# An adaLN block with linear attention and a gated feed-forward: a hand-interleaved kernel rewritten as a task graph ordered by a list scheduler

## Chip, cores and metric

One core of a Trainium2 chip. The metric is device time in microseconds (us) of one execution. Ratios in this text are the mean time of one kernel's fast runs over that of the other's of the same rounds, so not quite the ratio of the medians that are quoted. In the profile PE is TensorE, PEld its weight loads, DVE VectorE, ACT ScalarE, POOL GpSimd, SP SyncE.

## The reference, cut to what matters

```python
# x: (1, 2048, 512) bf16, 32 heads of 16, feed-forward width 1376
mod = silu(c) @ w_mod                                   # 6 vectors of 512: sa, ca, ga, sb, cb, gb
h   = layernorm(x) * (1 + ca) + sa
q, k, v = split(h @ wqkv)
pq, pk  = q @ w_phi, k @ w_phi                          # per head, 16x16
phi_q   = concat(softmax(pq), softmax(-pq))             # 32 features per head
phi_k   = concat(softmax(pk), softmax(-pk))
kv, z   = phi_k.T @ v, sum(phi_k)                       # over all 2048 positions
o   = (phi_q @ kv) / (phi_q @ z + 1e-6)
x   = x + ga * (o @ wo)
h   = layernorm(x) * (1 + cb) + sb
x   = x + gb * ((sigmoid(h @ w_gate) * (h @ w_up)) @ w_down)
```

kv needs every position, so no output tile can start before all 16 tiles (128 rows each) have been through K, V and phi. That cuts the kernel into stages: A, loads and preparation; B, the key/value pass over 16 tiles; C, the way from kv to the first gate matmul; D, the feed-forward part, during which the later tiles still pass through attention.

Names in the profiles: xn is a normalised tile, h1T and h2T its transposes with scale and shift; kvbd is kv laid out for the matmuls; sm, m, den and cc are the steps from phi_q @ z to the factor that divides, num is phi_q @ kv, u the divided num; a_ps is the product with `wo`, tg the tanh of gate, hm its product with up, y the product with `w_down`. To evict is to copy a result out of PSUM, TensorE's output memory of eight banks.

## The kernel before

`w_phi` is folded into the weights of q and k at the start; `ga` is multiplied into `wo`, and `gb` into `w_down`, on the chip. Everything is emitted in an order fixed by hand. Stage B is a loop over tiles with the preparation of the next group of four tiles woven in:

```python
    for i in range(NT):
        g, j = i // 4 + 1, i % 4
        k_v(i)                                   # V matmuls of tile i
        k_vaug(i)                                # ACT: evict V
        if j == 0 and g < 4:
            for t in range(4 * g, 4 * g + 4):
                ln1_xn(t)                        # DVE: normalise the next group
        k_k(i)                                   # K matmuls of tile i
        if g < 4:
            ln1_quarter(g, j, 7, on_dve=False)   # 4 TensorE transposes, ACT eviction
        # ... (cut)
        k_exp(i)                                 # ACT: exp(k), exp(-k)
        if i >= 3:
            k_kv(i - 3, kvacc, vaug[(i - 3) % VS])
        if i >= 1 and g < 3:
            ln_stats(x_sb[:, 4 * g + 4 + j, :], st1, mv1, 4 * g + 4 + j)
            if j == 3:
                ln_rstd(slice(4 * g + 4, 4 * g + 8), mv1, ve1, rs1)   # POOL
        # ... (cut)
        k_norm(i)                                # DVE: sum, reciprocal; POOL: phi
```

In stage D, chunks of 2, 2, 4, 4 and 4 tiles go through gate and up. Gate has PSUM bank 0 and up bank 1 (two of each in the first chunk), y banks 2 and 3, attention 4 to 7. After each slice of 128 features, a fixed number of y matmuls of the chunk before is issued, then those attention steps whose hand-set time has come:

```python
        for k, ct in enumerate(CHUNKS):
            # ... (cut)
            for ft in range(FT):
                gb_, ub_ = ((0, 1) if ft % 2 == 0 else (2, 3)) if k == 0 else (0, 1)     # (shortened)
                # gate matmuls -> ACT tanh -> up matmuls -> DVE hm
                if k == 0 and first:
                    wd_scale(ft)                 # POOL: gb into w_down
                # ... y matmuls of the chunk before: `per` of them
                run_events()                     # attention steps that are due
```

## Time and profile before

| | before |
|---|---|
| median of 4 runs beside the changed kernel | 281.55 us (281.06 to 281.93) |
| profiled span | 279.7 us |
| stage B ends (last kvacc matmul) | 85.1 us |
| first gate matmul | 110.8 us |
| last y done (last output addition starts) | 274.2 us |

How to read the page: the first part gives each engine's busy time in the span; the second cuts the span into 40 slices (7 us each here) and gives the busy share of each in tenths. PEclk is the clock granted to TensorE in tenths. These are lines of both parts for the kernel before:

```profile
span 279.7 us, 3972 instructions
PE 223.1 (80%) x1494; PEld 122.1 (44%) x1494; DVE 171.2 (61%) x330; ACT 104.9 (38%) x197; POOL 77.0 (28%) x85
...
PE   0959679399786757768777958999769899999992
...
DVE  2576876747358494869677866476957445942420
...
POOL 3432725727570040645722040103120100000000
PEclk9986959779999997979999999999999999999998
```

Where stage B ends is read from the timeline (start, length, then engine, line, operation, tiles, count); these are the eight kvacc matmuls of the sixteenth tile:

```profile
84.48 0.64 PE L245 MATMUL kvacc<-vaug,phi 128*128 128x136 bf16 x8
```

TensorE's row has 6s and 7s up to three quarters of the span, and its clock falls to 5 to 7 in several slices. The windows, the chain and the waits of this kernel are in the prediction.

### The profile page before, as it was taken

To read this page: it belongs to the slowest core of one execution; us is meant where nothing else is said; L and a number is where in the kernel's file an instruction comes from. 1 tells how busy PE (TensorE), PEld (TensorE's weight loads), DVE (VectorE), ACT (ScalarE), POOL (GpSimd) and SP (SyncE) were. 2 spreads that over 40 slices of the span, in tenths; PEclk is the share of its full clock that TensorE was granted. 3 is DMA by queue.
4 is the path that set the end of the run, shared out by engine and by line. 5 is a ranking of instruction groups with operands and counts; after the bars stand their busy time and mean duration, and the time that the engine had idled before them with its cause. 6 is when DMAs were issued, how large, how long until landed. Compare 5 with 4: busy or idle time off the path is not lost.

```text
span 279.7 us, 3972 instructions
## 1 busy us (share of the span) xinstructions
PE 223.1 (80%) x1494; PEld 122.1 (44%) x1494; DVE 171.2 (61%) x330; ACT 104.9 (38%) x197; POOL 77.0 (28%) x85
## 2 busy tenths in 40 slices
PE   0959679399786757768777958999769899999992
PEld 0814336155443434645455643445424344444440
DVE  2576876747358494869677866476957445942420
ACT  2637538168674534334443122431131322122100
POOL 3432725727570040645722040103120100000000
PEclk9986959779999997979999999999999999999998
DMA  7999900000000000001111203021022100000011
GB/s 201 397 290 406 363 6 1 0 0 2 0 1 2 0 0 2 0 5 35 39 38 23 73 2 95 0 56 41 0 55 57 40 20 19 19 21 19 20 57 45
DMA packets 23178, 17.14 MB, mean 61 GB/s; under 512 B 15617, under 2 KB 20594, under 8 KB 23154
## 3 DMA queue, kind: packets, MB, share of 16 engines
q1 hardware_dynamic: 23120, 16.82, 19.2%
q8 instruction: 13, 0.21, 0.3%
q14 instruction: 11, 0.09, 0.1%
q0 software_dynamic: 32, 0.02, 0.1%
q10 hardware_dynamic: 2, 0.00, 0.0%
HBM read 11.06 MB, written 2.10 MB: 47 GB/s over the span
## 4 chain that ended last, share of the span: by engine, by line
PE 54%; DVE 18%; issue 7%; POOL 6%; ACT 6%; DMA 5%; SPq 2%; POOLq 0%; DVEq 0%; ACTq 0%
PE y_ps L570 10%; PE g_ps L597 9%; PE u_ps L602 9%; PE v_ps L218 5%; PE k_ps L223 4%; PE a_ps L428 4%; PE q_ps L253 4%; PE kvacc L245 3%; DVE st L130 3%; DMA wp_sb<-in_A_w_phi_dram 2%; PE tp_h L147 2%; POOL phi L239 2%; DVE u L402 2%; POOL rs L135 2%; DVE xn L141 2%
## 5 line engine op out<-in xcount | busy, mean ns | idle before, releaser
L603 DVE SCALAR_TENSOR_TENSOR hm<-tg,u_ps 128x512 bf16<-128x512 bf16 (+3 forms) x55 | 31.7, 577 | 46.2 <-PE u_ps L602 33.2
L599 ACT ACTIVATE tg<-g_ps 128x512 bf16<-128x512 f32 (+3 forms) x55 | 28.0, 509 | 70.7 <-PE g_ps L597 68.3
L597 PE MATMUL g_ps<-h2T,wg_sb 128*128 128x512 bf16 (+3 forms) x220 | 47.5, 339 | 5.0 <-ACT tg L599 4.9
L602 PE MATMUL u_ps<-h2T,wu_sb 128*128 128x512 bf16 (+3 forms) x220 | 47.1, 337 | 4.3 <-DVE hm L603 4.1
L570 PE MATMUL y_ps<-wd_sb,hm 128*128 128x512 bf16 (+1 forms) x176 | 45.3, 379 | 0.0
L239 POOL TENSOR_TENSOR phi<-e,kr 128x1024 bf16<-128x1024 bf16 x16 | 30.8, 1927 | 29.9 <-DVE kr L237 21.8
L597 PEld LDWEIGHTS <-wg_sb 128*128 128x128 bf16 (+1 forms) x220 | 21.5, 101 | 24.0 <-issue 7.4
L602 PEld LDWEIGHTS <-wu_sb 128*128 128x128 bf16 (+1 forms) x220 | 21.9, 100 | 21.5 <-issue 5.3
L235 DVE TENSOR_REDUCE ksum<-e 128x64 f32<-128x1024 bf16 x16 | 19.3, 1208 | 18.0 <-ACT e L231 18.0
L409 POOL TENSOR_TENSOR o<-u,u 128x512 bf16<-128x512 f32 x12 | 15.2, 1266 | 44.4 <-DVE u L402 42.4
L570 PEld LDWEIGHTS <-hm 128*128 128x128 bf16 (+1 forms) x176 | 17.2, 98 | 18.4
L256 ACT ACTIVATE eT<-q_ps 128x512 bf16<-128x512 f32 x32 | 17.4, 595 | 16.9 <-PE q_ps L253 16.9
L428 PE MATMUL a_ps<-wo_sb,oT 128*128 128x512 bf16 x64 | 17.3, 394 | 7.5 <-ACT eT L256 2.6
L402 DVE TENSOR_TENSOR u<-num,cc 128x512 f32<-128x512 f32 (+1 forms) x32 | 20.4, 681 | 0.8 <-PE num L400 0.6
L218 PE MATMUL v_ps<-wv_sb,h1T 128*128 128x512 bf16 x64 | 20.1, 445 | 0.0
L134 POOL TENSOR_SCALAR ve<-mv 128x2 f32<-128x2 f32 (+1 forms) x12 | 2.7, 224 | 59.8 <-DVE mv L131 59.8
L152 ACT ACTIVATE h1T<-tp_h,modc 128x512 bf16<-128x512 bf16 x14 | 10.9, 779 | 21.8 <-PE tp_h L147 21.7
L223 PE MATMUL k_ps<-wqk_f,h1T 128*128 128x512 bf16 x64 | 19.0, 426 | 0.0
L147 PE MATMUL tp_h<-ident,xn 128*128 128x128 bf16 x64 | 9.6, 266 | 11.6 <-DVE xn L141 11.1
L253 PE MATMUL q_ps<-h1T,wqk_f 128*128 128x512 bf16 x64 | 18.2, 410 | 0.0
L231 ACT ACTIVATE e<-k_ps 128x512 bf16<-128x512 f32 x32 | 17.2, 595 | 0.2 <-PE k_ps L223 0.2
L447 ACT ACTIVATE xn<-x,nmr,rs 128x512 bf16<-128x512 f32 x12 | 9.4, 807 | 19.3 <-DVE nmr L440 19.3
(94 smaller groups left out, 269.0 us busy)
## 6 DMA issues: line engine op xcount, KB each, us to landing
x_sb<-in_A_x_dram SPq DMA_DIRECT2D x4, 512.0 KB, 9.8
wmod_sb<-in_w_mod_dram SPq DMA_DIRECT2D x1, 2048.0 KB, 8.7
out_dram<-ot SPq DMA_DIRECT2D x16, 128.0 KB, 1.7
wg_sb<-in_B_w_gate_dram SPq DMA_DIRECT2D x1, 1376.0 KB, 12.5
wu_sb<-in_B_w_up_dram SPq DMA_DIRECT2D x1, 1376.0 KB, 15.4
wd_sb<-in_B_w_down_dram SPq DMA_DIRECT2D x1, 1280.0 KB, 15.5
wmod_sb<-in_w_mod_dram SPq DMA_DIRECT2D x1, 1024.0 KB, 8.0
wk_sb<-in_A_wqkv_dram SPq DMA_DIRECT2D x1, 512.0 KB, 5.7
```

Of the source, the lines that this page charges most:

```text
L218: pe.matmul(v_ps[t][:], lhsT=h1T[:, j, t * P:(t + 1) * P], rhs=wv_sb[:, j, :], start=(j == 0), stop=(j == KT - 1))
L223: pe.matmul(k_ps[t][:], lhsT=h1T[:, j, t * P:(t + 1) * P], rhs=wqk_f[:, j, D:2 * D], start=(j == 0), stop=(j == KT - 1))
L235: dve.tensor_reduce(sm[:], e_t[t][:], axis=AX.X, op=ALU.add)
L239: pool.tensor_tensor(phi_t[t][:], e_t[t][:], r[:].unsqueeze(3).to_broadcast([P, 2, H, DH]), op=ALU.mult)
L253: pe.matmul(ps[:], lhsT=wqk_f[:, j, blk * P:(blk + 1) * P], rhs=h1T[:, j, cq * 512:(cq + 1) * 512], start=(j == 0), stop=(j == KT - 1))
L402: dve.tensor_tensor(u[:], ps[:].rearrange("p (h d) -> p h d", d=DH), c_t[p][:, q, s, :].unsqueeze(2).to_broadcast([P, H, DH]), op=ALU.mult)
L428: pe.matmul(ps[:], lhsT=o[:, j, :], rhs=wo_sb[:, j, :], start=(j == 0), stop=(j == KT - 1))
L570: yield lambda y=y, ft=ft, fsz=fsz, tl=tl: pe.matmul(y[:], lhsT=hm[k][:fsz, ft, tl * P:(tl + 1) * P], rhs=wd_sb[:fsz, ft, :], start=(ft == ...
L597: pe.matmul(g_ps[:fsz, 0:n], lhsT=wg_sb[:, j, ft * P:ft * P + fsz], rhs=h2T[k][:, j, 0:n], start=(j == 0), stop=(j == KT - 1))
L599: act.activation(tg[:fsz, 0:n], g_ps[:fsz, 0:n], ACT.Tanh, scale=0.5)
L602: pe.matmul(u_ps[:fsz, 0:n], lhsT=wu_sb[:, j, ft * P:ft * P + fsz], rhs=h2T[k][:, j, 0:n], start=(j == 0), stop=(j == KT - 1))
L603: dve.scalar_tensor_tensor(hm[k][:fsz, ft, 0:n], tg[:fsz, 0:n], 1.0, u_ps[:fsz, 0:n], op0=ALU.add, op1=ALU.mult)
```

## The change

The intent is to replace the hand-made order by a computed one. Every operation becomes a task with inputs, outputs, buffers, a duration per engine that may run it and a due time. A list scheduler simulates the five engines and, at each moment, gives a free engine the ready task that is due first. PSUM banks are one pool of eight: a task whose banks are not free reserves them. Cut to its core (the diff touches nearly the whole file):

```diff
-CHUNKS = [2, 2, 4, 4, 4]
+CHUNKS = [1, 1, 2, 4, 4, 4]
+UNITS = [[0], [1]] + [[t, t + 1] for t in range(2, NT, 2)]
+SPLIT = 14
+    def order(self):
+        # due times are passed back along the dependencies, then:
+            ready.sort(key=lambda t: (t.due, t.i))
+            for t in list(ready):
+                engs = [e for e in t.alts if free_at[e] <= now + 1e-9]
+                # ... (cut)
+                if any(len(slots[c]) < n or c in held for c, n in need.items()):
+                    held.update(need)             # reserve the banks it lacks
+                    continue
+                e = min(engs, key=lambda e: t.alts[e])
+    CAPS = {"bank": 8, ...}
 # stage B: tiles 8 to 15 (g > 1) get xn on ACT or POOL and DMA transposes
+            G.add(f"xn1_{t}", {"DVE": 0.25 + 0.1 * g} if g < 2 else {"ACT": 0.81, "POOL": 0.8}, ...)
+            if g > 1:
+                G.add(f"xT1_{t}", {"SP": 0.1}, lambda e, t=t, xn=xn: sp.dma_start_transpose(...), ...)
 # the last two tiles: positive and negative half of phi are tasks of their own, on POOL or DVE
+        parts = [(0, 2)] if t < SPLIT else [(0, 1), (1, 2)]
 # stage D: y matmuls have a due time only; any bank
+                    due = gdue[k + 1, i * FT // nd] + 0.02 if k + 1 < NC else ydue + i * 0.216
+                    G.add(f"y{t}.{ft}", {"PE": 0.216}, f_y, r=[("hm", k, ft), ("wd", ft)], ...)
 # wo is scaled from a copy of ga in SBUF (before: from PSUM), on POOL or DVE
-        dve.tensor_tensor(wo_sb[:, j, :], wo_sb[:, j, :], gamod["ga"][:], op=ALU.mult)
+        G.add(f"wo{j}", {"POOL": 1.2, "DVE": 0.65}, lambda e, j=j: engine(e).tensor_tensor(wo_sb[:, j, :], wo_sb[:, j, :], ga_sb[:], op=ALU.mult), ...)
```

## The prediction

> **What bounds the kernel now.** I read the page's slices first: TensorE has neither a full row nor one cause of idling. The windows view, cut at stage borders I chose from the timeline, comes next (columns: window, its length, then busy time and instruction count of PE, weight loads, DVE, ACT, POOL, then granted clock, DMA share, GB/s):
> ```profile
> 14.00:86.20 72.20, 55.72 (x378) 29.93 (x376) 47.33 (x73) 42.36 (x78) 35.86 (x26) 0.86 0.31 104
> 86.20:110.80 24.60, 16.72 (x145) 9.45 (x146) 16.10 (x36) 10.40 (x20) 3.31 (x4) 0.93 0.01 1
> 110.80:220.00 109.20, 90.00 (x641) 52.16 (x640) 75.62 (x160) 35.53 (x70) 32.09 (x35) 0.98 0.14 33
> 220.00:274.20 54.20, 53.96 (x250) 24.51 (x249) 25.43 (x47) 10.30 (x18) 0.00 (x0) 1.00 0.09 30
> ```
> Stage B (14 to 86) is the key/value pass over 16 tiles, C (to 111) the latency until the first gate matmul, D1 (to 220) the feed-forward part while later tiles still pass through attention, D2 the last chunk. Only D2 is TensorE-bound. In B, C and D1 DVE is busy 66 to 69%, TensorE 68 to 82%: neither is full. The chain that ended last shows why in B:
> ```profile
> 31.19 1.93 POOL phi L239
> ...
> 33.39 1.05 POOL rs L135
> ...
> 34.47 2.11 DVE xn L141
> ...
> 37.88 0.91 PE kvacc L245 x8
> 38.79 1.71 PE v_ps L218 x4
> 40.50 1.71 PE k_ps L223 x4
> ...
> 43.12 0.86 PE v_ps L218 x4
> 43.98 0.86 PE k_ps L223 x4
> ```
> Every fourth tile the pass stops: rs waits behind phi on POOL, the four xn run as one block on DVE, the transposes wait for them, and then V and K run at half speed (1.71 against 0.86 us). Between stops, V starts 2.43 us apart (timeline: 42.95, 45.38, 47.80). The waits confirm the in-order stops in C and D1:
> ```profile
> DVE hm L603 <- PE u_ps L602: 33.2, 29, 1.9
> DVE x L430 <- PE a_ps L428: 9.1, 9, 3.3
> PE num L400 <- DVE u L402: 4.6, 6, 2.6
> PE u_ps L602 <- DVE hm L603: 4.1, 3, 1.7
> ```
> Note that engines take turns waiting for each other: that is ordering, not capacity.
>
> **What the Trainium skill says.** "TensorE: Matmul & The Clock Gate", section "What's actually happening": the array runs at half clock after an idle window of about 3.4 us and regains full clock after a similar busy one. The trace agrees: 1.71 against 0.86 us above, after a gap. Same page, "Wait — 56ns, not 53.3ns?": warm matmuls start 55.6 ns (128 columns) or 215.7 ns (512) apart, never under about 25 ns. Agrees: the last 48 y matmuls take 10.39 us, 216.5 ns each; 16 of sm add 0.39 us. "SBUF — State Buffer", section "SBUF: two separate sides": DVE and GpSimd share a port pair as a lock held for the instruction. Agrees: four xn take 1.73 us at 19.04 but 3.07 us at 34.47, beside phi. "Perfetto Trace Analysis", section "Optimization Strategy": with several regimes, interleave them. That is this change's intent.
>
> **The floor.** Streaming time, from these pitches: 512-column equivalents are gate/up 352, y 176, K, V, Q and output 256, ga and gb 8, so 792 x 0.2165 = 171.5 us; the narrow ones after the change (kv, num, fold, transposes) 360 x about 0.056 = 20; sm and modc 192 x 0.025 = 5. Sum 196.5 us, of a 279.7 us span. The gap of 83 us is all there is to win.
>
> **The change, part by part.** I read the new instruction order of each engine.
>
> *Removed and moved.* Tiles 8 to 15 go to h1T by DMA transposes, so 32 TensorE transposes vanish, 24 more go with only two tiles on the TensorE route; 88 narrower gate/up matmuls come. A 128-column gate matmul costs 55 ns and four weight loads hide (eight num take 0.61 us with 0.17 us latency, 55 ns each), so one-tile chunks cost TensorE nothing: same columns. 56 transposes x 0.055 = 3 us saved. Their extra ACT and DVE evictions: 22 pairs in place of 11, with a 256-wide tg 0.38 and hm 0.415 us now; I estimate 0.26 us each at 128, so +1.5 us each.
>
> *Stage A* keeps its chain (x load, statistics, xn, transposes, first K): 14 us again.
>
> *Stage B.* Of DVE's 47.3 us, the eight xn of tiles 8 to 15 leave for ACT and POOL (3.07+2.98 us); six h1T writes come (two of 0.54, four SBUF ones about 0.35: 2.5 us), three half phi (about 0.8 each: 2.4 us), and one of four wo goes (0.6). So 47.3-6.0+2.5+2.4-0.6 = 45.6 us. ACT: 32 e x 0.595, 16 vaug x 0.595, 7 h1T x 0.78, 4 folds, 5 xn x 0.8, 8 eT, ga and gb: about 46 us. POOL: 14.5 phi x 1.93, 4 rs x 1.27, and some: 38 us. TensorE about 44. Four engines are then near 45 us; the block stops go, since statistics are done a group ahead and xn sits on another engine. None of them can be kept full by a rigid order; I take 87%: 45.6/0.87 = 52.4 us. Stage B ends at 14+52.4 = 66.4 instead of 86.2: 20 us gained. This is the largest part.
>
> *Stage C.* To the first gate matmul DVE now does, in its order: kvz 0.55, kvn 1.5, four den groups (1.1, 1.1, 1.6, 1.6), four pairs of u (8 x 0.68), two x1 (1.4), statistics 0.87, xn 0.8, mod 0.35: 16.3 us, with waits for ACT and PE about 19. Against 24.6 now, 5.5 us gained, as one tile is prepared instead of two with three DVE-blocking pairs. First gate at 85.5.
>
> *Stage D.* TensorE work after the first gate: y 38.1, gate/up 76.2, 14 output projections x 0.87 = 12.1, num 4.4, sm 1.6, one Q 0.9, transposes 0.3: 133.6 us. Today's order has 140.3 after its first gate and takes 163.4 (110.8 to 274.2): 23 us of stalls. In the new order y matmuls fill instead of running two or four at a time, any of eight banks can be taken, and chunk 0 is only one tile. But DVE between stage B's end and the last chunk's first gate has today 16.1+75.6 = 91.7 us, and gets about 7 more (narrow hm, a ninth den group, the bound checks 6 us earlier): 99 us. TensorE's own time for that stretch is 19 us of stage C and 133.6 less the last chunk's gate/up (19.0) and the 61 y behind its first gate (13.2), so 101: 120 us; DVE would need 82%, which it never reached here (68% now). I choose stalls of 11 us, half of today's: 131 us, DVE at 76%.
>
> *End.* The last row, 5.5 us from the last y to the end, stays.
>
> Sum: 66.4+19+133.6+11+5.5 = 235.5 us span. The profiled run reports 281.57 for a 279.7 span: add 1.9. Predicted 237.4, say 237 us, 0.84 of today.
>
> **The rivals.**
> 1. *DVE becomes the bound of D1.* For it: every eviction, u, x1 and statistic sits there; 99 us of work in a 120 us stretch. Against: it has 8 to 14 us windows at 78% already (140 to 160: 15.67 of 20). If its share stays at 68%, the stretch takes 99/0.68 = 146 instead of 131 us: 252 us.
> 2. *A fixed order is too rigid.* The order comes from fixed durations without the half-clock spells or the port lock; a late instruction holds all behind it. Two places look dangerous: POOL has eleven wd scalings (13.1 us today, spread out) in one block between the last phi and the first rs2, so rs2 may be late by some us; and SP holds all h1T transposes ahead of the wg, wu and wd loads, which today start at 16 us and would start near 40. The loads take 12.5 to 15.5 us from issue to landing, so are there before 60, ahead of need. wd then starts POOL's block at about 64 and ends at 77; rs2 is wanted at about 77. If both go wrong, 8 to 12 us: 246 to 249.
> 3. *The schedule holds nearly as drawn.* The code's own due times want one K tile each 2.45 us, which is the free-running 2.43 seen now. With B at 92% (49.6 us) and 4 us of stalls: 235.5-2.8-7+1.9 = 228 us.
> 4. *Half-clock spells come back*, as gaps merely move. Today B's granted clock is 0.86. B's TensorE work of 44 us in 52 leaves no long gap except around the second group's transposes: 2 us at most either way.
>
> For no gain to appear, both B and D1 would have to fill with new waits. B's stop has a visible cause that the order removes, so I hold this unlikely.
>
> **Range and chances.** Rival 3 sets the near edge (228, a little under for luck), rivals 1 and 2 the far one (252, both together rarer). 80%: 226 to 250. 2% faster means under 276.3, 39 us away from my number, beyond even rivals 1 and 2 together (about 262). Faster 0.97, same 0.02, slower 0.01.
>
> **What would show it.** Right: V and K of 0.86 us nearly throughout; kvacc's last matmul at 64 to 69; first gate at 82 to 89; TensorE busy over 90% from there; DVE at 75% or more in the stretch; last 5 us unchanged; 1,526 matmuls. Wrong: a POOL wait of ve on DVE turning into DVE or PE waiting on rs2 behind wd (rival 2); gate matmuls waiting on DVE mod with DVE over 90% busy (rival 1); DMA transposes as the largest releaser of TensorE; stage B ending after 72 with ACT or POOL full.

## The result, and the profile after

The changed kernel takes 232.44 us, median of 4 runs (231.60 to 233.27), against 281.55; the ratio is 0.8256 (95% interval 0.8222 to 0.8291). It is correct. First the page of the changed kernel, its first two parts and the shares of the chain that ended last:

```profile
span 230.8 us, 4164 instructions
...
PE 206.3 (89%) x1526; PEld 117.6 (51%) x1526; DVE 172.3 (75%) x355; ACT 103.1 (45%) x207; POOL 82.4 (36%) x91
...
PE   0588798899889769999999999999999999999990
...
DVE  0689998759997998978999974958677988432430
...
POOL 6405599679499725323200620110430300000000
PEclk9999999999999967999999999999999999999998
...
PE 60%; ACT 0%; DVE 0%; issue 0%
```

From the sixteenth slice to the last but one TensorE is never under 90%, and the clock dips in one place only. The chain names one engine: in the last 60% of the span nothing but TensorE's own work set the end (before, it was PE 54%, DVE 18%, issue 7% and others).

Now the windows of the changed kernel, cut at its own stage borders (columns as in the prediction: window, length, then busy time and count of PE, weight loads, DVE, ACT, POOL, then clock, DMA share, GB/s):

```profile
0.00:14.00 14.00, 6.00 (x81) 5.75 (x82) 6.24 (x18) 6.52 (x13) 6.26 (x22) 1.00 0.86 293
14.00:69.90 55.90, 49.31 (x367) 26.76 (x365) 50.47 (x81) 43.75 (x84) 40.59 (x29) 1.00 0.55 163
69.90:90.90 21.00, 17.90 (x184) 11.90 (x183) 18.77 (x40) 11.02 (x25) 13.27 (x14) 0.84 0.04 8
90.90:191.80 100.90, 100.39 (x751) 58.51 (x748) 81.77 (x188) 35.25 (x77) 22.31 (x27) 1.00 0.22 48
191.80:224.50 32.70, 32.67 (x151) 14.65 (x151) 14.36 (x32) 6.56 (x11) 0.00 (x0) 1.00 0.06 22
```

Against before: A the same; B 55.9 us in place of 71.1 (14 to 85.1); C 20.3 (to the first gate at 90.2) in place of 25.7; D 134.3 in place of 163.4; the end 0.8 us longer. So B gave 15.2 us, C 5.3 and D 29.1 of the span's 48.9. In D TensorE is busy 133.1 of 133.6 us; before it was busy 144.0 of 163.4 (the last two windows of the prediction), so some 19 of the 29 us are idle time that went. An estimate of the rest, from the count of matmuls after the first gate times their pitch (some 138 us before, 133 after): about 5 us of work moved ahead of the gate, and about 5 us were matmuls that ran slower before. DVE works 82% of the stretch from the end of B to the last chunk, (18.77 + 81.77) of 121.9 us, and in D TensorE does not wait for it. The prediction drew the border of B and C of the kernel before at 86.2 us, 1.1 us after the last kvacc matmul; the table below uses the last kvacc matmul for all kernels.

The waits of the changed kernel, all engines (columns: who waited for whom; total, times, longest):

```profile
DVE wmod_sb L480 <- PE u_ps L471: 21.7, 17, 2.6
...
PE kvacc L278 <- POOL phi L725: 2.4, 4, 1.1
...
PE tpo L380 <- DVE u L369: 2.3, 2, 1.9
...
PE k_ps L706 <- ACT h1T L691: 0.8, 1, 0.8
```

`wmod_sb` is hm, which shares that buffer now. DVE waiting for up (21.7 us, 33.2 before) is harmless: it is the engine that is not the bound. What TensorE waits for after stage A is a few us, all but 0.5 us of it in B and C; its waits of before on num, hm and tg in stage D are gone.

### The profile page after: what moved, and what is told of

Same layout as the page of the kernel before. It is cut to its first block, busy times and chain, and to the rows that moved or that the text cites. A ratio compares the mean times of both kernels' runs of the same rounds, so it can differ in the third digit from the quotient of the medians.

```text
span 230.8 us, 4164 instructions
## 1 busy us (share of the span) xinstructions
PE 206.3 (89%) x1526; PEld 117.6 (51%) x1526; DVE 172.3 (75%) x355; ACT 103.1 (45%) x207; POOL 82.4 (36%) x91
## 3 DMA queue, kind: packets, MB, share of 16 engines
q1 hardware_dynamic: 30272, 18.91, 29.1%
## 4 chain that ended last, share of the span: by engine, by line
PE 60%; ACT 0%; DVE 0%; issue 0%
PE u_ps L471 17%; PE g_ps L471 17%; PE y_ps L491 16%; PE a_ps L396 6%; PE num L363 2%; PE sm L338 1%; ACT eT L772 0%; PE q_ps L767 0%; DVE ot L500 0%; PE tp_x L443 0%; PE bnd L526 0%
## 5 line engine op out<-in xcount | busy, mean ns | idle before, releaser
L475 ACT ACTIVATE tg<-g_ps 128x512 bf16<-128x512 f32 (+5 forms) x66 | 29.5, 454 | 70.1 <-PE g_ps L471 59.1
L480 DVE SCALAR_TENSOR_TENSOR wmod_sb<-tg,u_ps 128x512 bf16<-128x512 bf16 (+5 forms) x66 | 32.3, 503 | 25.8 <-PE u_ps L471 21.7
L491 PE MATMUL y_ps<-wd_sb,wmod_sb 128*128 128x512 bf16 (+1 forms) x176 | 44.4, 379 | 0.0
L725 POOL TENSOR_TENSOR phi<-e,ks 128x1024 bf16<-128x1024 bf16 (+1 forms) x15 | 28.3, 1898 | 11.3 <-DVE ks L730 5.0
L387 POOL TENSOR_TENSOR o<-u 128x512 bf16<-128x512 f32 x14 | 17.9, 1287 | 35.6 <-DVE u L369 33.9
L471 PE MATMUL g_ps<-wT_sb,wg_sb 128*128 128x512 bf16 (+3 forms) x132 | 27.0, 326 | 0.0
L471 PE MATMUL u_ps<-wT_sb,wu_sb 128*128 128x512 bf16 (+3 forms) x132 | 26.8, 326 | 0.0
L471 PE MATMUL u_ps<-wqk_sb,wu_sb 128*128 128x128 bf16 (+5 forms) x132 | 22.1, 290 | 0.5 <-ACT eT L772 0.5
L471 PE MATMUL g_ps<-wqk_sb,wg_sb 128*128 128x128 bf16 (+5 forms) x132 | 22.2, 290 | 0.0
L722 DVE TENSOR_REDUCE ks<-e 128x64 f32<-128x1024 bf16 (+1 forms) x18 | 19.0, 1064 | 2.2 <-ACT e L719 2.2
L706 PE MATMUL k_ps<-wqk_f,h1T 128*128 128x512 bf16 x64 | 16.2, 380 | 1.5 <-ACT h1T L691 0.8
```

Of the source, the lines that this page charges most:

```text
L387: G.add(f"o{t}", {"POOL": 1.3}, lambda e, ub=ub, o=o: pool.tensor_tensor(o[:], ub[0][:].rearrange("p h d -> p (h d)"), ub[1][:].rearrange( ...
L471: pe.matmul(ps[:fsz, 0:n], lhsT=w[:, j, ft * P:ft * P + fsz], rhs=h[:, j, 0:n], start=(j == 0), stop=(j == KT - 1))
L475: G.add(f"tg{k}.{ft}", {"ACT": 0.15 + n * 0.00088}, lambda e, tg=tg, g_ps=g_ps, fsz=fsz, n=n: act.activation(tg[:fsz, 0:n], g_ps[:fsz, 0:n ...
L480: dve.scalar_tensor_tensor(hm_all[:fsz, hm[k].slot, ft, 0:n], tg[:fsz, 0:n], 1.0, u_ps[:fsz, 0:n], op0=ALU.add, op1=ALU.mult)
L491: pe.matmul(y[:], lhsT=hm_all[:fsz, hm[k].slot, ft, tl * P:(tl + 1) * P], rhs=wd_sb[:fsz, ft, :], start=(ft == 0), stop=(ft == FT - 1))
L706: pe.matmul(kp[:], lhsT=h1T[:, j, t * P:(t + 1) * P], rhs=wqk_f[:, j, D:2 * D], start=(j == 0), stop=(j == KT - 1))
```

## The experiments

Twelve kernels ran. The first eight (e0 to e7) were on one chip, where the changed kernel itself took 232.21 us; e8 to e11 were on another. The changed kernel itself was not run on that other chip, so e8 to e11 are compared with it by their ratios to the kernel before. All were timed against the kernel before, 6 runs each (5 fast ones for e11). Stages are from the profiled run: end of B is the last kvacc matmul, D runs from the first gate matmul to the last output addition.

| run | time us | ratio to before | end of B | first gate | length of D |
|---|---|---|---|---|---|
| kernel before | 281.55 | 1 | 85.1 | 110.8 | 163.4 |
| changed kernel | 232.44 | 0.8256 | 69.9 | 90.2 | 134.3 |
| e0_same | 232.21 | 0.8300 | 71.1 | 90.4 | 134.8 |
| e1_y_slots | 249.02 | 0.8898 | 70.2 | 90.5 | 150.9 |
| e2_pairs | 234.17 | 0.8377 | 69.9 | 91.5 | 134.9 |
| e3_no_split | 235.94 | 0.8433 | 70.9 | 93.6 | 135.6 |
| e4_pe_transposes | 233.27 | 0.8334 | 70.4 | 89.7 | 135.3 |
| e5_stats_shifted (on before) | 273.14 | 0.9738 | 77.2 | 102.9 | 163.9 |
| e6_wd_one_column (wrong result) | 227.92 | 0.8137 | 69.5 | 84.9 | 134.9 |
| e7_half_pool | 229.98 | 0.8206 | 69.1 | 87.0 | 135.4 |
| e8_wo_one_column (wrong result) | 231.25 | 0.8223 | 69.2 | 88.2 | 135.4 |
| e9_fixed_banks | 237.16 | 0.8436 | 70.7 | 91.2 | 138.7 |
| e10_slots_and_banks | 244.19 | 0.8698 | 70.1 | 90.5 | 144.1 |
| e11_half_pool_wo | 230.85 | 0.8215 | 70.0 | 87.9 | 134.9 |

The last column is the most telling one: D is 134 to 136 us whenever its rules are those of the change, and longer only in the three runs that restrict y or the banks. Everything else moves where D begins.

**The measure.** The same kernel again:

> The changed kernel once more, unaltered, as the measure for the three that run beside it on the same chip. All theories: 231.5 to 233.3 us, 0.822 to 0.829 of the kernel before.

232.21 us, as expected. Its stage B ends 1.2 us later than in the first profile, with the same first gate: a border inside the kernel can vary by a us from run to run. So can the clock: in the first profile TensorE had one spell at half clock while it worked (82.5 to 89.3 us), here two of half that length (from 42.1 and from 83.0 us).

**Does y as a filler make the difference in stage D?**

```diff
+        for k in range(NC):                     # y tasks added after all gate/up tasks
...
+                    slot = [("up", k + 1, i * FT // nd)] if k + 1 < NC else []
-                    G.add(f"y{t}.{ft}", {"PE": 0.216}, f_y, r=[("hm", k, ft), ("wd", ft)], ...)
+                    G.add(f"y{t}.{ft}", {"PE": 0.216}, f_y, r=[("hm", k, ft), ("wd", ft)] + slot, ...)
```

> The changed kernel with one more dependency for each y matmul: it may not be issued before the up matmuls of the next chunk's slot that the kernel before interleaves it with, so that y can no longer run ahead as filler. Theory 1 (stage D loses its stalls because y, attention and gate/up matmuls fill each other's waits freely): TensorE idles again in stage D, 7 to 15 us in all after the first gate, and the time rises to 240 to 248 us. Theory 2 (the stalls went because of other parts: smaller first chunks, any of eight PSUM banks, attention done ahead): idle time stays under 3 us and the time under 235 us. Stages B and C unchanged within 1 us under both.

249.02 us: 16.8 us more than e0, nearly all of it in D (150.9 in place of 134.8). Theory 1, though the time is 1 us above its range. TensorE is idle 12.3 us after the first gate (1.6 in e0), within the 7 to 15 that it named. What waits now is TensorE at the start of chunks, for the input of the chunk (`wT_sb` and `wqk_sb` are its two buffers); these are waits of TensorE in e1:

```profile
PE u_ps L471 <- DVE wT_sb L450: 7.1, 2, 4.2
...
PE u_ps L471 <- DVE wqk_sb L450: 2.6, 1, 2.6
```

In the changed kernel y matmuls of the chunk before are run in these moments. The idle time is not the whole price. The same stretch of 20 us in the windows of e0 and then of e1 (column before the last two: the clock):

```profile
190.00:210.00 20.00, 19.63 (x91) 8.59 (x91) 11.31 (x30) 5.14 (x9) 0.00 (x0) 1.00 0.09 26
```

```profile
190.00:210.00 20.00, 15.09 (x60) 6.40 (x60) 10.04 (x34) 5.73 (x9) 1.86 (x4) 0.83 0.17 40
```

Fewer matmuls in less busy time, and at 0.83 of the clock. In D TensorE is busy 138.7 us in e1 and 133.2 in e0, for the same matmuls. So of the 16.2 us, 10.7 are idle time and 5.5 slower work; about 4 of these (an estimate) are two spells at half clock, from 130.7 and from 198.9 us, with 8.1 us of busy time in them; each begins in or just after one of the gaps.

**Do the banks matter?**

```diff
-                g_ps, u_ps = bank("g_ps"), bank("u_ps")
+                two = 2 * (ft % 2) if k == 0 else 0
+                g_ps, u_ps = bank("g_ps", allow=(two,)), bank("u_ps", allow=(two + 1,))
-                y = bank("y_ps")
+                y = bank("y_ps", allow=(2 + t % 2,))
 # all other banks downstream: allow=(4, 5, 6, 7); order() takes the first free bank allowed
```

> The changed kernel with the downstream PSUM banks by role, as in the kernel before: gate only in bank 0 and up only in bank 1 (0 to 3 for the first chunk), y in banks 2 and 3, all else in 4 to 7; ordered anew by the same scheduler. Theory 1 (free banks are what keeps TensorE from waiting for evictions of gate and up in stage D): TensorE idles 4 us or more after the first gate, time 235 to 240. Theory 2 (with y as filler a single bank is enough, because y matmuls run while gate and up are evicted): time within 1.5 us of 232.2.

237.16 us; by the ratios (0.8436 against 0.8300 and 0.8256) 4 to 5 us more than the changed kernel. D is 138.7 us, 4 more. Theory 1 by the time, but TensorE idles only 2.9 us after the first gate (1.6 in e0), not the 4 or more that it named, and about 1.7 us of the longer D (an estimate) is a spell of 3.4 us at half clock that begins at 91.3 us, in e0 before the gate. "Perfetto Trace Analysis", section "Matmul Optimizations", of the Trainium skill says to make sure that all eight PSUM banks are used. No run here tests that: the kernel before and e9 use all eight as well. What e9 tests is that none is tied to a role, and that is worth about 2%.

Both restrictions together:

> Both the y matmuls held to their slots and the PSUM banks fixed by role. With y in its slots alone the time was 249.0 (16 us of stage D's 23 us of stalls back). If fixed banks are the rest, and each costs by itself: 252 to 258. If the two stand for the same waits: 247 to 251, and what remains of the 23 us lies in the order of the attention work.

Neither: 244.19 us, less than with the slots alone. D is 144.1 us in the profile (which fell on the fastest run of 242.44). A restriction given to a list scheduler makes it plan everything anew, so such a run measures the restriction and the new plan together, and effects do not add up. What can be said: taking the freedom of y away costs 7 us (e9 to e10) or 17 us (e0 to e1), depending on the plan around it. With both freedoms gone about 9 of the stage's 29 us are back. The rest, among it the 5 us of TensorE work that moved ahead of the first gate, was not taken apart.

**Are the one-tile first chunks worth it?**

```diff
-CHUNKS = [1, 1, 2, 4, 4, 4]
-UNITS = [[0], [1]] + [[t, t + 1] for t in range(2, NT, 2)]
+CHUNKS = [2, 2, 4, 4, 4]
+UNITS = [[t, t + 1] for t in range(0, NT, 2)]
```

> The changed kernel with chunks of 2, 2, 4, 4, 4 tiles and tiles 0 and 1 taken through attention as a pair, so without the one-tile first chunks. Theory 1 (the one-tile first chunk starts the gate matmuls earlier, and DVE's work for one tile instead of two is what the start waits for): first gate 2.5 to 5 us later, time up by 2 to 4 us, 234.5 to 236.5. Theory 2 (stage C's length is set by what POOL's block of wd scalings does to DVE, and small groups pay the most for it): first gate later by under 2 us and time within 1 us, since the pair runs after the block. The narrow gate matmuls cost TensorE nothing under both: TensorE busy within 1 us of 206.

The time is up by 2.0 us, just short of theory 1's range of 234.5 to 236.5, the first gate by 1.1 us only, which is theory 2. Worth about 2 us; the run does not decide between the reasons. TensorE's busy time is 205.6 against 205.0 us, so the narrow gate matmuls are free as predicted.

**Is the split by sign worth it?**

```diff
-SPLIT = 14
+SPLIT = 16
```

> The changed kernel without the split by sign of the last two tiles in stage B, so that POOL does the whole phi of tiles 14 and 15. Theory 1 (the split shortens the tail of stage B): kvacc's last matmul 1 to 2.5 us later and the time up by 1 to 2.5 us. Theory 2 (the halves on DVE, 1.35 us each and not the 0.8 estimated because POOL works beside them, eat what the split saves): stage B's end and the time within 0.7 us of the changed kernel's.

Both missed. The last kvacc matmul does not move (70.9 against 71.1 in e0), yet the time rises by 3.7 us and the first gate by 3.2. The timeline shows what the split buys. First the start of POOL's block of eleven wd scalings in e0; then, in e3, DVE's kvbd behind its wait, and the same block (columns: start, length, engine, line, operation, tiles, count):

```profile
66.90 13.72 POOL L756 TENSOR_TENSOR wd_sb<-wd_sb,wmod_sb 128x512 bf16<-128x512 bf16 x11
```

```profile
70.64 0.47 DVE L295 SCALAR_TENSOR_TENSOR kvbd<-kvacc,bmask 128x24 bf16<-128x24 f32 x3 [3.83 <-PE kvacc L278]
...
69.53 12.37 POOL L756 TENSOR_TENSOR wd_sb<-wd_sb,wmod_sb 128x512 bf16<-128x512 bf16 x11
```

Without the split DVE has nothing to do for 3.83 us, POOL does one and a half phi more, its wd block starts 2.6 us later and ends 1.3 us later, further into DVE's chain of stage C. That this later block, rather than the changed order on TensorE, makes the 3.2 us is inferred, not isolated. A rival is the clock: in stage C of e3 TensorE is at half clock for 10.3 us (from 83.1), in e0 for 3.4.

**Is stage C set by DVE waiting for POOL?** The order of all engines stays; only the width of POOL's wd scaling changes.

```diff
-pool.tensor_tensor(wd_sb[:, ft, :], wd_sb[:, ft, :], gb_bc[:], op=ALU.mult)
+pool.tensor_tensor(wd_sb[:, ft, 0:1], wd_sb[:, ft, 0:1], gb_bc[:, 0:1], op=ALU.mult)
```

> The changed kernel with each of POOL's eleven wd scalings cut to one column, wrong on purpose; the order on all engines is the same. Theory 1 (DVE's small operations with two SBUF inputs wait for POOL's instruction of 1.28 us, and DVE's chain sets the length of stage C): m, den and cc of the first two tiles fall from 0.63, 1.05 and 0.73 us to under 0.3 each, the first gate comes 2.5 to 4.5 us earlier, time down by 2.5 to 4.5 us. Theory 2 (stage C is set by latencies between PE, ACT and DVE): m, den and cc get shorter but the first gate moves by under 1 us.

227.92 us, 4.3 less, first gate 5.5 us earlier: theory 1, a little over its range for the gate. Of the 5.5 us, 3.9 lie in stage C, and m, den and cc of the first two tiles are 3.8 us shorter together. The other 1.6 lie at the end of B, where the block has already begun: the last two half phi on DVE take 0.66 and 0.68 us in place of 1.17 and 1.65. And the useful form of the test, with right results:

```diff
 # wd in two halves of 256 columns; the full phi on POOL in its two halves of 512
-pool.tensor_tensor(wd_sb[:, ft, :], wd_sb[:, ft, :], gb_bc[:], op=ALU.mult)
+[pool.tensor_tensor(wd_sb[:, ft, c:c + 256], wd_sb[:, ft, c:c + 256], gb_bc[:, c:c + 256], op=ALU.mult) for c in range(0, D, 256)]
+                for s in range(a, b):
+                    engine(e).tensor_tensor(...[:, s:s + 1], ee[:, s:s + 1], ks[:, s:s + 1]..., op=ALU.mult)
```

> The changed kernel with each wd scaling, and each full phi on POOL, issued as two instructions of half the width, results unchanged. Theory 1 (DVE waits until the POOL instruction under way has ended): the waits halve, m, den and cc in POOL's block fall by 0.3 us or so each, stage B and C together 1 to 4 us shorter, time 228.5 to 231.5. Theory 2 (while both are in line DVE and POOL share in another way, so length of an instruction does not matter): those means stay within 0.1 us, and POOL's fixed cost for 26 more instructions makes the kernel 0 to 2 us slower.

229.98 us, 2.2 less than e0, theory 1; the intervals of the two ratios (0.8174 to 0.8238 and 0.8264 to 0.8336) do not overlap. The groups by shape show it (columns: tiles and shapes, count, busy us, mean ns). The full width in e0, one column in e6, halves in e7; in each the wd scaling on POOL and then den of the first two tiles on DVE, which runs beside it:

```profile
L756 POOL TENSOR_TENSOR wd_sb<-wd_sb,wmod_sb 128x512 bf16<-128x512 bf16 x11 | 13.7, 1280 | 0.0
...
L349 DVE TENSOR_TENSOR den<-m 128x32 f32<-128x32 f32 x2 | 2.1, 1054 | 0.1
...
L349 DVE TENSOR_TENSOR den<-m 128x64 f32<-128x64 f32 x7 | 1.6, 225 | 0.2
```

```profile
L756 POOL TENSOR_TENSOR wd_sb<-wd_sb,wmod_sb 128x1 bf16<-128x1 bf16 x11 | 3.0, 314 | 0.0
...
L349 DVE TENSOR_TENSOR den<-m 128x32 f32<-128x32 f32 x2 | 0.4, 192 | 0.1
```

```profile
L757 POOL TENSOR_TENSOR wd_sb<-wd_sb,wmod_sb 128x256 bf16<-128x256 bf16 x22 | 15.5, 741 | 0.0
...
L349 DVE TENSOR_TENSOR den<-m 128x32 f32<-128x32 f32 x2 | 1.1, 561 | 0.1
```

A 32-element addition takes 0.19 us alone, 1.05 beside POOL instructions of 1.28, and 0.56 beside instructions of 0.74. Its length follows the length of the instruction that POOL has under way. The third line shows that twice as large a den, away from the block, takes 0.23. This is the lock that the prediction cites from "SBUF — State Buffer": held for the whole instruction.

**Does the same lock set the pace of stage B?**

```diff
-engine(e).tensor_tensor(wo_sb[:, j, :], wo_sb[:, j, :], ga_sb[:], op=ALU.mult)
+engine(e).tensor_tensor(wo_sb[:, j, 0:1], wo_sb[:, j, 0:1], ga_sb[:, 0:1], op=ALU.mult)
```

> The changed kernel with the four scalings of wo (three on DVE, 4.36 us in one block beside two phi on POOL; one on POOL) cut to one column, wrong on purpose; the order on all engines is the same. Theory 1 (DVE at 90% sets the pace of stage B, so the 5 us it lost to sharing with POOL are the 3.5 us by which stage B ended late): kvacc's last matmul 2.5 to 4.5 us earlier, time down by 2 to 4 us. Theory 2 (stage B is a chain that passes through all engines, and DVE has slack of its own: the kernel with the old transposes had DVE at 99% there and ended stage B within half a us): kvacc's last matmul under 1.5 us earlier, time down by under 1.5 us.

231.25 us. By the ratios to before this is 0.4 to 0.9% under the changed kernel (0.8223 against 0.8256 and 0.8300), some 1 to 2 us, and stage B ends 0.7 to 1.9 us earlier: nearer to theory 2, but not clear of theory 1. And the edit removed less than it was to remove. The wo group before the change, in the changed kernel, and in e8:

```profile
L310 DVE TENSOR_TENSOR wo_sb<-wo_sb,ga_ps 128x512 bf16<-128x512 bf16 x4 | 2.5, 683 | 2.8 <-PE ga_ps L263 2.8
```

```profile
L751 DVE TENSOR_TENSOR wo_sb<-wo_sb,ga_sb 128x512 bf16<-128x512 bf16 x3 | 4.4, 1503 | 0.0
```

```profile
L751 DVE TENSOR_TENSOR wo_sb<-wo_sb,ga_sb 128x1 bf16<-128x1 bf16 x3 | 2.4, 862 | 0.0
```

A single column still takes 862 ns in the mean, and the profile books it as busy. One by one the three take 0.54, 0.15 and 1.90 us; the last starts and ends with a phi on POOL (55.95 to 57.88, and it ends at 57.90). The three full-width ones of the changed kernel show the same (line, tiles, count, then shortest, median and longest in ns):

```profile
L751 DVE TENSOR_TENSOR wo_sb<-wo_sb,ga_sb x3: 680/1412/2416, 54.6 to 58.3; 128x512 bf16<-128x512 bf16 x3
```

The one of 680 ns starts at 58.3 us, when POOL is idle, the other two beside phi. In the kernel before ga was read from PSUM, and POOL was idle during all four (683 ns). So the second SBUF input costs nothing by itself; what costs is to run beside phi. Whether the old form would have waited there too, no run shows. The wait goes both ways: the phi beside the second wo took 2.38 us in place of 1.93.

The other test of stage B, the old preparation of tiles 8 to 15:

```diff
-        if g > 1:            # DMA transposes, xn on ACT or POOL
+        if g > 3:            # never: xn on DVE, transposes on TensorE
```

> The changed kernel with tiles 8 to 15 prepared as in the kernel before: xn on DVE, 32 transposes on TensorE, and the evictions with scale and shift, instead of xn on ACT or POOL and DMA transposes. Theory 1 (taking xn off DVE and the transposes off TensorE is part of stage B's gain, since DVE at 90% sets its pace): kvacc's last matmul 3 to 6 us later, time up by 3 to 7 us over the changed kernel's 232.2. Theory 2 (stage B's gain came from the order alone, and the DMA transposes' waits of 6 us give back what they save): within 1.5 us.

233.27 us, 1.1 more: theory 2 (the intervals of the ratios of e4 and e0 overlap). Stage B in the windows of e0 and then of e4 (third pair: DVE):

```profile
14.00:70.00 56.00, 49.56 (x356) 26.81 (x359) 49.57 (x78) 42.77 (x83) 39.34 (x28) 0.97 0.56 163
```

```profile
14.00:70.00 56.00, 51.35 (x393) 28.96 (x398) 55.30 (x84) 43.30 (x82) 38.13 (x26) 1.00 0.42 145
```

DVE has 5.7 us more in the same 56 us, 99% busy, and the stage ends no later. So moving xn and the transposes away is not where stage B's 15 us came from. (Part of DVE's busy time is waiting, so 99% is not 99% work.)

**Could stage B have been had by moving a call?**

```diff
-            ln1_quarter(g, j, 7, on_dve=False)
+            for jj in ([], [0], [1], [2, 3])[j]:
+                ln1_quarter(g, jj, 7, on_dve=False)
```

> The kernel before with one move only: within each group of four tiles of stage B, the statistics of the next group are begun one tile later. If the stops of stage B come from the place of these calls in a fixed order, a shift of one tile moves them and changes the time by several us in one direction (3 to 10); if any fixed order of whole quarters has the same stops, the time stays within 2 us of the kernel before. It tells whether the 16 us of stage B could have been had by moving calls; neither outcome speaks for the list scheduler by itself.

The expectation names the edit wrongly: what moves one tile later is the transposes and evictions of the next group, not its statistics. The time falls by 2.6%, to 273.14 us, 7 us and so the first outcome; stage B ends 7.9 us earlier, and everything after it keeps its length. The two stops of TensorE in the timeline, before and then in e5 (in brackets: idle time and what ended it):

```profile
36.62 1.26 PE L147 MATMUL tp_h<-ident,xn 128*128 128x128 bf16 x4 [3.24 <-DVE xn L141]
...
54.30 1.26 PE L147 MATMUL tp_h<-ident,xn 128*128 128x128 bf16 x4 [4.61 <-DVE xn L141]
```

```profile
34.69 0.88 PE L147 MATMUL tp_h<-ident,xn 128*128 128x128 bf16 x3 [0.99 <-DVE xn L141]
...
48.30 1.26 PE L147 MATMUL tp_h<-ident,xn 128*128 128x128 bf16 x4 [2.23 <-DVE xn L141]
```

In the old place the transposes stood in TensorE's queue behind the V and K of the very tile in which DVE begins the xn that they wait for. One tile later a further V and K stand before them. A single moved call gives half of what stage B gained (7.9 of 15.2 us): that half is order, not capacity.

**A faster version?**

> A candidate for a faster version: POOL's wd and phi in halves, as in the run of 229.98 us, and the scalings of wo in halves too, on either engine; results unchanged. If DVE's waits for POOL in the wo block matter for the time: 228.3 to 229.5. If not: 229.7 to 230.7.

230.85 us, just above the band for "no effect", ratio 0.8215 against 0.8206 for e7: wo in halves adds nothing. The best version with right results is e7, 1% under the changed kernel on the same chip (0.8206 to 0.8300).

## Why the prediction was right, point by point

232.4 us was measured and 237 predicted; the range and the direction hold. That the number came so near is in part luck: up to the first gate the kernel took 4.8 us more than the sum, in D 10.3 us less, at the end 0.8 more. Two of the prediction's own signs were missed by about 1 us (last kvacc matmul at 69.9 for 64 to 69, first gate at 90.2 for 82 to 89). The steps:

- **Stage B** was to end at 66.4 us and ends at 69.9 (69.1 to 71.1 over the runs on the changed kernel). The gain is 15.2 us (16.3 from the prediction's border) for 20. The named cause, stops made by the fixed order, is shown for half of it by e5; the three spells at half clock of the stage (mean clock 0.86) are gone in the first profile (1.00), with one of 3.4 us in e0 (0.97). The working, however, was 45.6 us of DVE work at 87%, with 6 us of xn leaving DVE as its largest term. DVE had 50.5 us at 90%, and e4 shows that putting xn back costs 1 us: the sum came near the right length by luck, for a reason that does not hold. The terms that were too small: half phi on DVE 1.35 us each for an estimated 0.8; wo 1.50 for 0.6. Both wait for POOL: where its instructions are short or absent they take 0.66 to 0.68 us (e6, and the last wo).
- **Stage C** was to take 19 us to the first gate, starting from the end of B, and took 20.3, a gain of 5.3 us (4.3 from the prediction's border) for 5.5. It would have been about 4 us shorter but for POOL's wd block (e6). The prediction used its m, den and cc from the kernel before and did not ask what would run beside them.
- **Stage D**: TensorE's work after the first gate was worked out as 133.6 us; the measured length is 134.3. The mis-sized term is the stalls, 11 us chosen as half of before's; they are under 1 us. (The 140.3 us of work named for the kernel before come to some 138 in a recount from its trace.) "DVE would need 82%, which it never reached here" was the wrong measure: it reached 82%. A share seen under one order is not a limit under another. y as filler (7 to 17 us) and free banks (4 to 5 us of the whole time) are the parts shown to matter.
- **Matmul count and evictions**: 1,526 matmuls as predicted, one-tile chunks free for TensorE (e2).
- **The end** took 6.3 us for an expected 5.5.

**Rivals.** Rival 1, DVE as the bound of D: refuted, TensorE is busy 133.1 of 133.6 us. Rival 2 named the right place with the wrong mechanism: rs2 was not late (POOL sat idle 5.7 us before the first one, in both profiles of the changed kernel), but the wd block cost 4.3 us through the lock. (The rival did say that the fixed durations leave the lock out.) The late loads did no harm: in the two profiles of the changed kernel POOL's wd block does not wait for them. Rival 3, the schedule holding nearly as drawn, came nearest for D. Rival 4, half-clock spells moving elsewhere: in the first profile they left B, and one of 6.8 us stands in C (0.84), which costs at most half its length, 3.4 us, for the 2 us estimated; e0 has two of 3.4 us, the profiles of e4 and e7 none before the last y.

**Still open**: what of D's other gain comes from the order of the attention work, and what of stage B's remaining 7 us comes from which part (the split is worth 3.7 us of the whole time, the new preparation 1).

## What to carry to other kernels

When several engines are each two thirds busy and take turns waiting, the order may be the bound, as here: look for instructions queued right behind what they wait for, and give the engine that should be full a supply of independent work that may run at any time. Don't take an engine's busy share under the old order as its limit, and remember that busy time on VectorE includes waiting for GpSimd. Before GpSimd gets a block of work, see which VectorE operations with two SBUF inputs will run beside it, and cut the block into shorter instructions. Look at other VectorE work too: in the kernel before, xn, with a single tensor input, took 2.10 us beside phi and 0.40 without.

## What the Trainium skill lacked or had wrong

- "SBUF — State Buffer" describes the lock, but not that a VectorE instruction's time in the profile contains the wait; "Perfetto Trace Analysis", section "DVE / Act Engine Instruction (TENSOR_ADD, Activation, etc)", which says where that time begins and ends, does not place the lock in it. Here den, 0.19 us alone, shows 1.05 us beside GpSimd instructions of 1.28 us, and a one-column product shows 0.15 to 1.90.
- The first of these pages does not give the remedy that the runs show: halving GpSimd's instructions took den to 0.56 us and the kernel down by 1%.
